# Making the marks of the attention on ScalarE, and other steps for GpSimd's splits in the first expert tile

## The chip, the cores and the metric

One core of a Trainium2 chip runs the kernel. The metric is the device time of one execution in microseconds (us). Engines: TensorE (PE; its weight loads are PEld), VectorE (DVE), ScalarE (ACT), GpSimd (POOL) and SyncE (SP), which issues DMAs. Each takes its instructions in order.

## What is computed

Three stages on B = 4 sequences of 768 tokens, 3072 tokens in all, 384 values each (8 heads of 48), all in float32: a linear attention, a mixture of 8 experts of which every token uses one, and a dense layer.

```python
for t in range(S):                               # attention
    cur = einsum('bhd,bhe->bhde', u[None] * kt, vt)
    y[:, :, t] = einsum('bhd,bhde->bhe', rt, state + cur)
    state = wt[:, :, :, None] * state + einsum('bhd,bhe->bhde', kt, vt)
...
logits = x @ w_gate + modality_bias[modality_id] # experts
e_idx = argmax(logits, axis=1)
gate_w = softmax(logits)[arange(N), e_idx]
h = maximum(x[mask] @ w1[e], 0.0)
out[mask] = gate_w[mask, None] * (h @ w2[e])
...
h = x @ w_in                                     # dense layer
out = (h * clip(h + 3.0, 0.0, 6.0) / 6.0) @ w_out
```

## The kernel before

**Attention (0 to about 187 us).** A loop over 24 steps i, each a chunk of 128 tokens of one sequence (c is the chunk in its sequence, 0 to 5). In step i TensorE forms the products of the pairs (`pairs_a`, line 830, tile aps), the new state (`update`, lines 861 and 865) and the output of the step before (`pairs_y`, 884 and 890; `take_y`, 898). VectorE prepares step i + 1 ahead of it (`prep_scan`, 775 to 779, and `prep_mult`, 788 and 789, tiles kt and pt), which TensorE's first product of step i + 1 reads. ScalarE copies: masks a_sb (837), k by tokens (kk, 851), heads and state (869, 873), the output x (899), its transpose xT (723), and it scales x by its gate before it is stored (711). GpSimd masks (839) and makes two products (z, 801, and av, 814). A few small matmuls of line 688 only fill gaps. Every engine's order is the order in which the program issues its instructions.

**Routing.** The 24 chunks form five groups (6, 6, 5, 3 and 4 chunks). Some steps after the last chunk of a group, `between()` chooses its experts (`choose`), counts, finds each token's place (`place`; plo, line 349, is its place within a row of 112) and makes the marks (`mark`, line 355): for chunk t a table of 128 tokens by 112 places, ohv, that is 0 except at the token's place, where it is the token's code (its number less 1536, plus one from the middle on, so that no code is 0; code_c). The first three groups, 17 chunks, are marked in the attention on VectorE: group 0 in steps 11 (two) and 12 (four), group 1 in steps 17, 18 and 19 (two each), group 2 in steps 22 (two) and 23 (three). `mark` is issued after the copies of k and of the factors a (`tokens_k`, `own_a`) and ahead of `take_y` and of the transposes in the same step. A matmul of the marks with a table of rows (ohh, 128 by 24 x 60, made by the large comparison of line 445) gives the index of the token in each slot: line 409 for the first expert tile, line 463 for all (24 matmuls into one sum), after which line 464 writes idx_x. The last two groups are finished within the first expert tile, by `routing_end`, a generator that is taken a step further at fixed places; there GpSimd marks five chunks and VectorE two.

**Expert tiles (about 187 to 400 us).** Seven tiles of 448 slots. Each has 8 steps f: `first(f)` (9 matmuls, tile hps, then the hidden values on ScalarE, line 589, and their rests on VectorE, line 590, tiles ring), then, two steps late, `second(f - 2)` (9 matmuls, tile acc, the third, sixth and ninth with w2l), then `side(f)`. A weight is used as a high and a low part; `split` (514, 515) makes them: a copy on ScalarE and a subtraction on VectorE or GpSimd. The table `splits` says which blocks are split in which step: in it "15" is block 5 of w1, "23" block 3 of w2. w1's block f is wanted by first(f), w2's block f by second(f). In the first tile `side(f)` issues, in this order: the routing's next step (f = 0, 1, 3), the four gathers of the next tile's tokens on GpSimd (f = 3; line 554, they read idx_x), and the splits of the step. The raw weights of the next expert are loaded into a half as soon as the half is split (line 251).

**Dense layer (to the end).** Six tiles of 512 tokens; nothing of the change lies there.

Of the kernel before, what the change touches and what calls it, by code (L numbers as in the profile page):

```python
# [9 lines left out]
F32 = mybir.dt.float32  # L10
# [5 lines left out]
AF = mybir.ActivationFunctionType  # L16
ALU = mybir.AluOpType
# [15 lines left out]
NTK = NT // 128  # L33
TM = 448
SUB = 112
NSUB = TM // SUB
# [3 lines left out]
NSLOT = NT_MAX * NSUB  # L40
# [10 lines left out]
HALF = NT // 2  # L51
# [18 lines left out]
def attention_moe_ffn(ctx, tc, wkr, v_tok, v_t, u, modality_id, w_gate, modality_bias, w1, w2, w_in, w_out, out):  # L70
    nc = tc.nc
    PE, ACT, DVE, POOL, SP = nc.tensor, nc.scalar, nc.vector, nc.gpsimd, nc.sync
    ctx.enter_context(tc.manual_schedule())

    const = ctx.enter_context(tc.tile_pool(name="const", bufs=1))
# [50 lines left out]
    iota_c = iota("iota_c", [128, SUB], [[1, SUB]], 1)  # L126
    slot_c = iota("slot_c", [128, NSLOT], [[1, NSLOT]])

    code_c = iota("code_c", [128, NTK], [[128, NTK]], -HALF, 1)
    POOL.tensor_scalar(out=code_c[:, NTK // 2:], in0=code_c[:, NTK // 2:], scalar1=1.0, scalar2=None, op0=ALU.add)  # L130
    wg_sb = const.tile([128, KD, E], F32, name="wg_sb")

    logit = keep.tile([128, NTK, E], F32, name="logit")
# [123 lines left out]
    R = {}  # L257
# [17 lines left out]
    class Route:  # L275
# [76 lines left out]
        def mark(self, js, engine):  # L352
            for j in js:
                t = self.t0 + j
                engine.tensor_scalar(out=R["ohv"][:, t, :], in0=iota_c, scalar1=self.plo[:, j:j + 1],
                                     scalar2=code_c[:, t:t + 1], op0=ALU.is_equal, op1=ALU.mult)

# [48 lines left out]
        def first_rows(self, ps):  # L406
            m = self.s.stop
            for i in range(m):
                PE.matmul(ps[0:SUB, 0:NSUB], lhsT=R["ohv"][:, i, :], rhs=self.fohh[:, i], start=(i == 0), stop=(i == m - 1))
            DVE.tensor_scalar(out=idx_x[:, 0:NSUB], in0=ps[0:SUB, 0:NSUB], scalar1=float(HALF), scalar2=None, op0=ALU.add)  # L410

        def finish(self, ps):

# [15 lines left out]
            half = self.m // 2  # L429
# [28 lines left out]
                              op1=ALU.mult)  # L458
            DVE.scalar_tensor_tensor(out=texp, in0=tef, scalar=float(E - 1), in1=own, op0=ALU.min, op1=ALU.add)
            yield  # L460
            ips = ps[0:SUB, 128:128 + NSLOT]
            for i in range(NTK):
                PE.matmul(ips, lhsT=R["ohv"][:, i, :], rhs=ohh[:, i], start=(i == 0), stop=(i == NTK - 1))
            DVE.tensor_scalar(out=idx_x, in0=ips, scalar1=float(HALF), scalar2=None, op0=ALU.add)
            yield
            after = self.tile([SUB, NSLOT], "after")
# [275 lines left out]
    with ExitStack() as actx:  # L742
# [189 lines left out]
        for i in range(n):  # L932
# [6 lines left out]
            def between():  # L939
                for part in parts:  # L940
                    at = i - part.s.stop - 3
                    if at == 0:
                        part.choose()
                    if at == 1 or (at == 0 and i == n - 1):
                        part.gates()
                        to_store.extend(range(part.s.start, part.s.stop))
                    if at == 1:
                        part.steps = part.place()
                        next(part.steps)
                        next(part.steps)  # L950
                        part.add_counts()
                    if at == 2:
                        for _ in part.steps:
                            pass
                        part.mark(range(2), DVE)
                    if at == 3:
                        part.mark(range(2, 4 if part is early else part.m), DVE)
                    if at == 4 and part is early:
                        part.mark(range(4, part.m), DVE)

            if i in (n - 4, n - 3):
                w_load(0, i - (n - 4))
# [86 lines left out]
    def routing_end():  # L1049
# [20 lines left out]
        for i in range(last.s.start, last.s.stop):  # L1070
# [6 lines left out]
    banks(pctx, reuse_waits="tile")  # L1077


    splits = {(0, 0): "22", (0, 1): "14", (0, 2): "15 23", (0, 3): "16 24", (0, 4): "17 25", (0, 5): "26",  # L1080
# [3 lines left out]
    loads = {(0, 3): 0, (0, 6): 1, (1, 2): 0, (1, 5): 1}  # L1084
# [264 lines left out]
```

## Time and profile before

| | |
|---|---|
| median of 3 runs | 825.85 us (824.87 to 825.90) |
| the profiled execution, its span | 825.67 us, 824.0 us |
| TensorE busy, of the span | 797.4 us, 97% |
| VectorE | 520.1 us, 63% |
| ScalarE | 376.8 us, 46% |
| GpSimd | 227.2 us, 28% |

The profile is one execution. A busy share is a mean over stages, so the stretches are read one by one. A row of the timeline gives the start in us, the time in us, the engine, the line, the operation, the tiles written and read and how many instructions of the kind follow each other; in brackets stands how long the engine had been idle before it, and what ended that. The granted clock is TensorE's, as a share of its full 2.4 GHz; its other level is 1.2 GHz.

### The profile page before, as it was taken

To read this page: it belongs to the slowest core of one execution; us is meant where nothing else is said; L and a number is where in the kernel's file an instruction comes from. 1 tells how busy PE (TensorE), PEld (TensorE's weight loads), DVE (VectorE), ACT (ScalarE), POOL (GpSimd) and SP (SyncE) were. 2 spreads that over 40 slices of the span, in tenths; PEclk is the share of its full clock that TensorE was granted. 3 is DMA by queue.
4 is the path that set the end of the run, shared out by engine and by line. 5 is a ranking of instruction groups with operands and counts; after the bars stand their busy time and mean duration, and the time that the engine had idled before them with its cause. 6 is when DMAs were issued, how large, how long until landed. Compare 5 with 4: busy or idle time off the path is not lost. (4 is left out here: it accounts for less than half of the span.)

```text
span 824.0 us, 16170 instructions
## 1 busy us (share of the span) xinstructions
PE 797.4 (97%) x6456; PEld 696.3 (85%) x6481; DVE 520.1 (63%) x924; ACT 376.8 (46%) x801; POOL 227.2 (28%) x240
## 2 busy tenths in 40 slices
PE   9999999999999999999999899999999999999993
PEld 4677777778999999999999799999999999999992
DVE  7789999977588989887279843433433333333331
ACT  3556677675455555554344433333333333333331
POOL 9566565655524314311012220020010002002001
PEclk9999999999999999999999999999999999999997
DMA  6797577832879877474543310110100001001001
GB/s 162 137 314 160 120 140 160 241 104 74 206 212 231 183 266 224 138 245 131 115 151 94 116 39 1 39 39 1 34 26 20 1 1 39 0 1 39 1 1 42
DMA packets 50832, 87.49 MB, mean 106 GB/s; under 512 B 11130, under 2 KB 34747, under 8 KB 50747
## 3 DMA queue, kind: packets, MB, share of 16 engines
q1 hardware_dynamic: 45147, 74.81, 33.5%
q0 software_dynamic: 4640, 11.51, 4.9%
q8 instruction: 53, 0.87, 0.5%
q14 instruction: 32, 0.26, 0.1%
q10 hardware_dynamic: 960, 0.05, 0.1%
HBM read 65.38 MB, written 20.97 MB: 105 GB/s over the span
## 5 line engine op out<-in xcount | busy, mean ns | idle before, releaser
L511 PE MATMUL hps<-xin,wih 128*128 128x512 f32 x576 | 179.1, 392 | 0.0
L632 DVE SCALAR_TENSOR_TENSOR r<-r,hps 128x512 f32<-128x512 f32 (+1 forms) x97 | 66.1, 681 | 164.5 <-ACT r L631 164.5
L511 PE MATMUL acc<-woh,ring 128*128 128x384 f32 x576 | 163.9, 339 | 2.2 <-DVE ring L636 2.2
L631 ACT ACTIVATE r<-hps,three 128x512 f32<-128x512 f32 (+1 forms) x97 | 66.3, 683 | 167.2 <-PE hps L511 166.7
L511 PEld LDWEIGHTS hps<-xin,wih 128*128 128x128 f32 x576 | 106.8, 188 | 17.7
L511 PE MATMUL hps<-xin,wil 128*128 128x512 f32 x288 | 113.9, 396 | 0.0
L671 POOL DMA_INDIRECT out<-zo,order x24 | 24.8, 1033 | 315.5 <-ACT zo L668 310.0
L511 PEld LDWEIGHTS acc<-woh,ring 128*128 128x128 f32 x576 | 105.5, 188 | 7.4 <-DVE ring L636 3.2
L636 DVE SCALAR_TENSOR_TENSOR ring<-r,ring 128x512 fp32r<-128x512 f32 (+1 forms) x97 | 67.0, 691 | 59.2 <-ACT ring L635 59.1
L511 PE MATMUL hps<-xin,w1h 128*128 128x448 f32 x336 | 98.2, 373 | 0.0
L511 PE MATMUL acc<-wol,ring 128*128 128x384 f32 x288 | 96.9, 336 | 0.0
L511 PE MATMUL acc<-ring,w2h 128*128 128x448 f32 x336 | 95.8, 366 | 0.0
L635 ACT ACTIVATE ring<-r 128x512 fp32r<-128x512 f32 (+1 forms) x97 | 60.7, 626 | 64.0 <-DVE r L632 64.0
L515 POOL TENSOR_TENSOR w2l<-w2r,w2h 128x384 fp32r<-128x384 f32 x33 | 36.9, 1123 | 126.3 <-ACT w2h L514 126.3
L511 PEld LDWEIGHTS acc<-ring,w2h 128*128 128x128 f32 x336 | 63.5, 189 | 4.7
L511 PEld LDWEIGHTS hps<-xin,w1h 128*128 128x128 f32 x336 | 61.8, 189 | 4.2 <-DVE xin L563 0.2
L511 PE MATMUL tps<-woh,ring 128*128 128x384 f32 x192 | 64.0, 334 | 0.0
L511 PEld LDWEIGHTS hps<-xin,wil 128*128 128x128 f32 x288 | 54.0, 187 | 11.5
L511 PE MATMUL hps<-xin,w1l 128*128 128x448 f32 x168 | 61.5, 366 | 0.0
L511 PE MATMUL acc<-ring,w2l 128*128 128x448 f32 x168 | 61.3, 365 | 0.0
L589 ACT ACTIVATE ring<-hps 128x448 fp32r<-128x448 f32 x56 | 30.4, 543 | 63.1 <-PE hps L511 62.9
L511 PEld LDWEIGHTS acc<-wol,ring 128*128 128x128 f32 x288 | 54.1, 188 | 4.1
(237 smaller groups left out, 1347.7 us busy)
## 6 DMA issues: line engine op xcount, KB each, us to landing
wkr<-in_wkr SPq DMA_DIRECT2D x42, 288.9 KB, 5.0
w1r<-in_w SPq DMA_DIRECT2D x14, 768.0 KB, 6.1
w2r<-in_w SPq DMA_DIRECT2D x14, 768.0 KB, 8.3
raw<-in_w_in SPq DMA_DIRECT2D x12, 512.0 KB, 8.1
raw<-in_w_out SPq DMA_DIRECT2D x16, 384.0 KB, 3.1
yt_dram<-yst SPq DMA_DIRECT2D x7, 672.0 KB, 7.3
v_sb<-in_v_tok SPq DMA_DIRECT2D x24, 192.0 KB, 5.6
yt_dram<-warm_sb SPq DMA_DIRECT2D x3, 1536.0 KB, 9.6
```

The source lines that it names most:

```text
L511: PE.matmul(ps, lhsT=lt, rhs=rt, start=(start and q == 0), stop=(stop and q == last))
L515: sub.tensor_tensor(out=l, in0=raw, in1=f32(h), op=ALU.subtract)
L589: ACT.activation(out=hh, in_=ps, func=AF.Relu)
L631: ACT.activation(out=r6[:, s], in_=ps[:, s], func=AF.Relu, bias=three)
L632: DVE.scalar_tensor_tensor(out=r6[:, s], in0=r6[:, s], scalar=6.0, in1=ps[:, s], op0=ALU.min, op1=ALU.mult)
L635: ACT.activation(out=gh[:, s], in_=r6[:, s], func=AF.Copy, scale=1.0 / 6.0)
L636: DVE.scalar_tensor_tensor(out=gl[:, s], in0=r6[:, s], scalar=1.0 / 6.0, in1=f32(gh[:, s]), op0=ALU.mult, op1=ALU.subtract)
L671: ins = POOL.indirect_dma_start(out=out[:, :], out_offset=bass.IndirectOffsetOnAxis(ap=order[:, s:s + 1], axis=0), in_=zo, in_offset=None, ...
```

## The change

The marks of the attention are made on ScalarE: the square of the distance of the token's place from each column, then max(0, code - code x square), which is the code at distance 0 and 0 elsewhere. This needs positive codes, so the codes of the first half of the tokens change sign (code_c) and a table of negative codes is added (code_n), both made by GpSimd ahead of its other work. The sign is put back where codes are read: line 410 multiplies by -1; in `finish` the 24 matmuls form two sums, one for each half of the tokens, one is copied, and their difference is the index. In the first expert tile the splits move to other steps: "14 22" in step 0, none in steps 1 and 2, "15 23" in step 3, and the later ones one step on. `split_w1` there uses GpSimd for f < 3 and VectorE afterwards, as before, so w1's block 5 goes from GpSimd to VectorE.

```diff
 
     code_c = iota("code_c", [128, NTK], [[128, NTK]], -HALF, 1)
     POOL.tensor_scalar(out=code_c[:, NTK // 2:], in0=code_c[:, NTK // 2:], scalar1=1.0, scalar2=None, op0=ALU.add)
+
+    POOL.tensor_scalar(out=code_c[:, :NTK // 2], in0=code_c[:, :NTK // 2], scalar1=-1.0, scalar2=None, op0=ALU.mult)
+    code_n = const.tile([128, NTK], F32, name="code_n")
+    POOL.tensor_scalar(out=code_n, in0=code_c, scalar1=-1.0, scalar2=None, op0=ALU.mult)
     wg_sb = const.tile([128, KD, E], F32, name="wg_sb")
 
     logit = keep.tile([128, NTK, E], F32, name="logit")
...
         def mark(self, js, engine):
             for j in js:
                 t = self.t0 + j
+                if engine is ACT:
+
+                    far = self.pool.tile([128, SUB], F32, name="far", bufs=1)
+                    ACT.activation(out=far, in_=iota_c, func=AF.Square, scale=-1.0, bias=self.plo[:, j:j + 1])
+                    ACT.activation(out=R["ohv"][:, t, :], in_=far, func=AF.Relu, scale=code_n[:, t:t + 1],
+                                   bias=code_c[:, t:t + 1])
+                    continue
                 engine.tensor_scalar(out=R["ohv"][:, t, :], in0=iota_c, scalar1=self.plo[:, j:j + 1],
                                      scalar2=code_c[:, t:t + 1], op0=ALU.is_equal, op1=ALU.mult)
 
...
             m = self.s.stop
             for i in range(m):
                 PE.matmul(ps[0:SUB, 0:NSUB], lhsT=R["ohv"][:, i, :], rhs=self.fohh[:, i], start=(i == 0), stop=(i == m - 1))
-            DVE.tensor_scalar(out=idx_x[:, 0:NSUB], in0=ps[0:SUB, 0:NSUB], scalar1=float(HALF), scalar2=None, op0=ALU.add)
+            DVE.tensor_scalar(out=idx_x[:, 0:NSUB], in0=ps[0:SUB, 0:NSUB], scalar1=-1.0, scalar2=float(HALF), op0=ALU.mult,
+                              op1=ALU.add)
 
         def finish(self, ps):
 
...
                               op1=ALU.mult)
             DVE.scalar_tensor_tensor(out=texp, in0=tef, scalar=float(E - 1), in1=own, op0=ALU.min, op1=ALU.add)
             yield
-            ips = ps[0:SUB, 128:128 + NSLOT]
+            half = [ps[0:SUB, o:o + NSLOT] for o in (128, 256)]
             for i in range(NTK):
-                PE.matmul(ips, lhsT=R["ohv"][:, i, :], rhs=ohh[:, i], start=(i == 0), stop=(i == NTK - 1))
+                PE.matmul(half[i >= NTK // 2], lhsT=R["ohv"][:, i, :], rhs=ohh[:, i], start=(i % (NTK // 2) == 0),
+                          stop=(i % (NTK // 2) == NTK // 2 - 1))
+            low = self.tile([SUB, NSLOT], "low")
+            DVE.tensor_copy(low, half[0])
+            ips = self.tile([SUB, NSLOT], "ips")
+            DVE.tensor_tensor(out=ips, in0=half[1], in1=low, op=ALU.subtract)
             DVE.tensor_scalar(out=idx_x, in0=ips, scalar1=float(HALF), scalar2=None, op0=ALU.add)
             yield
             after = self.tile([SUB, NSLOT], "after")
...
                     if at == 2:
                         for _ in part.steps:
                             pass
-                        part.mark(range(2), DVE)
+                        part.mark(range(2), ACT)
                     if at == 3:
-                        part.mark(range(2, 4 if part is early else part.m), DVE)
+                        part.mark(range(2, 4 if part is early else part.m), ACT)
                     if at == 4 and part is early:
-                        part.mark(range(4, part.m), DVE)
+                        part.mark(range(4, part.m), ACT)
 
             if i in (n - 4, n - 3):
                 w_load(0, i - (n - 4))
...
     banks(pctx, reuse_waits="tile")
 
 
-    splits = {(0, 0): "22", (0, 1): "14", (0, 2): "15 23", (0, 3): "16 24", (0, 4): "17 25", (0, 5): "26",
-              (0, 6): "27 10 11", (0, 7): "12 13 20",
+    splits = {(0, 0): "14 22", (0, 1): "", (0, 2): "", (0, 3): "15 23", (0, 4): "16 24", (0, 5): "17 25",
+              (0, 6): "26 27 10 11", (0, 7): "12 13 20",
               (1, 0): "21 22 14", (1, 1): "23 15", (1, 2): "16 24", (1, 3): "17 25", (1, 4): "26 10", (1, 5): "27 11 20",
               (1, 6): "12 21", (1, 7): "13 22", (2, 0): "23 14 24"}
     loads = {(0, 3): 0, (0, 6): 1, (1, 2): 0, (1, 5): 1}
```

## Rows read from the trace of the kernel before

**Rows 1.** Busy us of each engine in a stretch, granted clock, DMA share
```profile
100.00:160.20 60.20, 55.94 (x1122) 43.42 (x1130) 58.32 (x103) 41.49 (x114) 37.32 (x37) 1.00 0.73 162
```

**Rows 2.** Timeline, TensorE, its waits for VectorE in the attention
```profile
107.01 0.71 PE L830 MATMUL aps<-pt,kt 48*128 48x128 f32 x8 [0.87 <-DVE pt L789]
...
144.43 0.71 PE L830 MATMUL aps<-pt,kt 48*128 48x128 f32 x8 [0.93 <-DVE pt L789]
...
150.96 0.71 PE L830 MATMUL aps<-pt,kt 48*128 48x128 f32 x8 [0.67 <-DVE pt L789]
...
159.65 0.38 PE L688 MATMUL ups<-warm_sb 128*128 128x512 bf16 x1 [0.81 <-DVE idx_x L410]
```

**Rows 3.** Timeline, VectorE, two groups of marks
```profile
137.51 0.58 DVE L355 TENSOR_SCALAR ohv<-iota_c,plo,code_c 128x112 f16<-128x112 f32 x2
...
150.73 2.16 DVE L355 TENSOR_SCALAR ohv<-iota_c,plo,code_c 128x112 f16<-128x112 f32 x2
```

**Rows 4.** ScalarE by form to 187 us: count, busy us, mean ns, idle before
```profile
L711 ACT ACTIVATE x_keep<-x_keep,gate 128x384 f32<-128x384 f32 x19 | 10.9, 608 | 0.0
...
L514 ACT ACTIVATE w1h<-w1r 128x384 fp32r<-128x384 f32 x2 | 1.0, 515 | 0.0
...
L300 ACT ACTIVATE ex<-lsub 128x24 f32<-128x24 f32 x1 | 0.2, 223 | 0.0
```

**Rows 5.** Busy us of each engine in two stretches around later marks
```profile
174.08:186.73 12.65, 12.65 (x233) 9.96 (x236) 7.03 (x21) 10.46 (x28) 4.44 (x6) 1.00 0.25 82
135.43:151.10 15.67, 13.93 (x284) 10.50 (x288) 15.19 (x29) 11.06 (x28) 10.54 (x12) 1.00 0.78 169
```

**Rows 6.** Timeline, the end of the attention on ScalarE and TensorE
```profile
176.21 1.61 ACT L711 ACTIVATE x_keep<-x_keep,gate 128x384 f32<-128x384 f32 x3
...
186.73 0.49 ACT L899 ACTIVATE x_keep<-yps 128x384 f32<-128x384 f32 x1
...
187.64 0.49 PE L720 MATMUL tps<-ident,x_keep 128*128 128x128 f32 x3
```

**Rows 7.** Timeline, places of group 1, and a copy that TensorE reads
```profile
136.72 0.75 DVE L349 SCALAR_TENSOR_TENSOR plo<-phw,rsel 128x6 f32<-128x6 f32 x1
...
149.33 0.55 ACT L851 ACTIVATE kk<-tps 128x448 f32<-128x448 f32 x1
...
152.11 0.67 PE L865 MATMUL ups<-v_sb,kk 128*64 128x48 f32 x16
```

**Rows 8.** Timeline, GpSimd and VectorE at the start
```profile
4.14 1.13 POOL L130 TENSOR_SCALAR code_c<-code_c 128x12 f32<-128x12 f32 x1
...
5.26 1.77 DVE L777 TENSOR_SCALAR tot<-pt 112x4 f32<-112x4 f32 x1
```

**Rows 9.** Timeline, the first expert tile around the large comparison
```profile
195.28 1.28 DVE L355 TENSOR_SCALAR ohv<-iota_c,plo,code_c 128x112 f16<-128x112 f32 x2
...
197.88 1.99 POOL L515 TENSOR_TENSOR w1l<-w1r,w1h 128x384 fp32r<-128x384 f32 x2
...
198.06 0.87 DVE L443 SCALAR_TENSOR_TENSOR phi<-phi,phw 128x24 f32<-128x24 f32 x1
...
198.97 2.42 DVE L445 TENSOR_TENSOR ohh<-slot_c,phi 128x1440 f16<-128x1440 f32 x1
...
201.43 1.38 PE L463 MATMUL tps<-ohh,ohv 128*112 128x60 f16 x24 [1.46 <-DVE ohh L445]
```

**Rows 10.** Busy us and granted clock behind the comparison, and in the dense layer
```profile
202.00:208.00 6.00, 6.00 (x35) 5.52 (x34) 3.91 (x11) 1.37 (x3) 2.88 (x4) 0.72 0.42 146
...
500.00:600.00 100.00, 100.00 (x503) 90.57 (x502) 37.71 (x56) 35.16 (x56) 4.19 (x4) 1.00 0.08 24
```

**Rows 11.** Timeline, the index, GpSimd behind the gathers, and second(3)'s third matmul
```profile
204.26 0.20 DVE L464 TENSOR_SCALAR idx_x<-tps 112x60 int32<-112x60 f32 x1
...
209.57 2.97 POOL L515 TENSOR_TENSOR w2l<-w2r,w2h 128x384 fp32r<-128x384 f32 x3
...
210.19 0.36 PE L511 MATMUL acc<-ring,w2l 128*128 128x448 f32 x1
```

## Prediction, made before the changed kernel was run

> **What bounds the kernel now.** I read the engine table and the slices first: TensorE is busy for 97% of the span, so only three kinds of time can be won: TensorE's waits, its slow clock, and work of its own. The change touches no TensorE work but a split of one sum. Then I read the busy times by stretch, in which TensorE and VectorE are both nearly full in the second half of the attention [rows 1]: two engines in step, so an idle moment of TensorE there is VectorE being late. The timeline names these moments: four waits of TensorE on VectorE between 100 and 160 us, 0.87, 0.93, 0.67 and 0.81 us, together 3.28 us [rows 2]. All other iterations there run at TensorE's own pace. The second place is the first expert tile: TensorE waits 1.46 us for the large comparison, and a stretch at a lower clock follows [rows 9, 10]. After about 220 us TensorE is full, and nothing of the change lies there.
>
> A forecast is made against the profiled execution: 825.67 us, a span of 824.0 and 1.67 around it; the median of the runs is 825.85, so the two are the same within 0.2 us. What a measurement of this kernel can tell from no change is about 0.2%, 1.65 us.
>
> **Marks leave VectorE.** 17 marks (6, 6 and 5 tokens' tiles in three groups) go. Two of them take 0.58 us when GpSimd leaves VectorE alone and 2.16 us when it doesn't [rows 3]. The excess is a wait which the next VectorE instruction may inherit, so I count 0.29 us a mark for sure: 17 x 0.29 = 4.9 us of VectorE. It is worth only what TensorE waited for, at most 3.28 us: each of the four waits has marks of 0.58 us or more among the instructions of VectorE in the one or two iterations ahead of it, and with those gone VectorE comes early enough for most of each. Bounds: 0.58 us each where the freed time goes into another wait for GpSimd (four times, 2.3 us, or as little as 1 us if the late ones inherit it), and 3.28 us.
>
> **Marks come to ScalarE.** The trace has no such instruction, so I build one: 24 columns take 223 ns and 384 take 515 ns, 0.81 ns a column, so 112 columns take 294 ns; a scale per partition adds 608 - 515 = 93 ns [rows 4]. Square has one such operand (387 ns), Relu two (480 ns): 0.87 us a mark. Neighbours on ScalarE overlap by (3 x 0.608 - 1.61) / 2 = 0.11 us [rows 6], but Relu reads what Square writes. I take 0.85 (0.65 to 0.87). That is 17 x 0.85 = 14.5 us for the 4.9 us taken off VectorE.
>
> The Trainium skill speaks against such an exchange: in "ScalarE: Activation LUTs", Rules for kernel authors, plain arithmetic belongs on VectorE. Its section What ACT_TABLE_LOAD costs gives 186 ns + 0.833 ns a column + 93 ns per pointer operand, by which a mark would take an estimated 0.84 us less an overlap; the rows above agree.
>
> Does ScalarE have room? It is a queue in order, so I look where marks stand and what is behind them. Group 0 (two, then four marks): ScalarE idles there and nobody waits soon; nothing. Group 1: the first two marks wait for the places, which VectorE finishes at 136.72 + 0.75 = 137.47 us, while ScalarE is free for them from 135.43: 2.04 us of standing, with four marks by 151.1 that is 2.04 + 3.4 = 5.4 us against 15.67 - 11.06 = 4.6 us of idle time [rows 5, 7]. Behind them stand the copies of x, the masks and the copy of k; that copy ends at 149.88 and TensorE takes it at 152.11, a slack of 2.2 us [rows 7]. 0.8 of it goes to the lateness and 1.6 to TensorE's own two gains there (0.93 + 0.67): 0.2 short. Not all idle time can be used, so I take 0.5 us off the gain (0 to 1).
>
> Group 2 is worse. Its five marks fall in the last two iterations: 5 x 0.85 = 4.25 us, against 12.65 - 10.46 = 2.19 us of idle time on ScalarE from 174.08 to 186.73 [rows 5]. So ScalarE ends the attention 2.06 us late. Behind the marks stand the copies of the last x, the first x to be split and the transposed x; the last copy of x ends at 187.22 and TensorE transposes it at 187.64 [rows 6], a slack of 0.2 to 0.4. So TensorE loses **1.8 us** there (0.6 at 0.65 us a mark, 2.3 if the idle time is poorly used). VectorE had nothing late there, so nothing is won against it.
>
> **GpSimd's two constants.** Two more small instructions stand ahead of the memsets. Alone such ones take about 0.2 us; the one there now takes 1.13 us beside a scan, and a VectorE instruction of four elements takes 1.77 us until the memsets are over [rows 8]. Behind them on GpSimd's queue stand the bias of the router, the first product z (own_z) and the first masks, for which TensorE's first iteration waits. I take 0.5 us (-0.5, if VectorE slips in between the two dependent instructions, to 1.2, if one is held like its neighbour).
>
> **Code sums.** The two sums are 24 matmuls as before; two VectorE instructions of 60 columns are added ahead of the index, of some 0.2 us each, as the index itself takes [rows 11]. The gathers wait for them, and what waits for the gathers is below.
>
> **The first tile.** Now VectorE's chain meets GpSimd's subtractions: an instruction of 24 columns takes 0.87 us and ends as the first subtraction does, and the comparison takes 2.42 us, beginning while the second runs to 199.87 [rows 9]. Without them they would end about 0.7 + 0.9 us sooner. Against that: one more weight copy (0.4 to 0.5 us) now stands ahead of the copy of the hidden values on ScalarE (ring, line 589), which VectorE's chain follows; and the two subtractions of the first step now run back to back while VectorE's own two marks (1.28 us beside one subtraction [rows 9]) want to start, up to 0.8 us more. So the comparison ends between 200.2 and 201.2 instead of 201.39, and the wait of 1.46 us shrinks to between 0.3 and 1.25.
>
> The Trainium skill, "GPSIMD Engine Reference", Specifications, says that GpSimd shares its SBUF interfaces with VectorE, and that instructions with two SBUF inputs contend. The trace agrees for the subtractions; by that rule GpSimd's own marks, which now end near 199, would hold the chain too, and the wait would be the long one.
>
> The clock that falls behind the wait (a mean of 0.72 granted from 202 to 208, between its two levels) cost some 6 x (1 - 0.72) = 1.7 us [rows 10]. That may go. But the subtraction of w2's block 3 now stands on GpSimd behind the four gathers, which wait for the index and occupy GpSimd until 209.57 [rows 11]; the index, and they, come 0.3 to 1.1 us earlier after the change, so block 3's subtraction, 1 us, ends at 209.4 to 210.2. TensorE wants it in the third matmul of second(3), at 210.19 before [rows 11]. With wait and slow clock gone it would be there sooner: the sums end at 201.6 to 202.5, then 9 + 9 + 9 + 2 matmuls of 100 / 503 = 0.2 us [rows 10] make 207.4 to 208.3. So a new wait of about 1.9 us takes the place of the old one and takes most of the gain back; I keep **0.4 us** of gain (3.1 if the wait did not come, a loss of 1.5 if the clock falls behind it as well). The block's raw weights are also freed later for the next load, which has some 10 us.
>
> **Sum.** -3.3 + 0.5 + 1.8 + 0.5 - 0.4 = -0.9: 825.67 - 0.9 = **824.8 us**.
>
> **Rivals.** (1) *The marks are cheap*: Square and Relu overlap or idle time takes them, 0.6 us lost at the end instead of 1.8, nothing at the start, and the slow clock goes for 1.1 us more: about 822.0. For it: ScalarE is the least full of the three in the attention. Against: the last two iterations. Chance 0.33.
> (2) *Slower through block 3*: the wait behind the gathers is long enough for the clock to fall again. This decides once TensorE arrives over 1.5 us ahead of the subtraction, since the wait of 1.46 us was followed by the slow clock [rows 9, 10]. The tile then loses 1.5 instead of gaining 0.4, and with ScalarE's end at 2.3 and the start at 1.2 the time is 825.67 - 2.8 + 2.3 + 1.2 + 1.5 = 827.9. For it: the order on GpSimd's queue. Against: GpSimd may get its indices earlier. Chance 0.20.
> (3) *VectorE gains nothing*: the freed time is inherited as waits for GpSimd, 1 us won instead of 3.3, the rest as in the sum: 827.1. For it: the marks' times of 2.16 against 0.58. Against: the 0.58 themselves. Chance 0.10.
> My forecast has 0.37.
>
> **Chances and range.** Faster by over 0.2% is below 824.2: rival 1 and a small part of the forecast, 0.37. Slower is above 827.5: most of rival 2 and a part of 3, 0.22. The same: 0.41. The range holds the ends of the terms of the forecast, most of rival 1 and up to rival 2: 821.6 to 828.0.
>
> **What would show it.** In the profile after: no wait of TensorE on VectorE's prepared tiles after 100 us (right) or the same four (rival 3); ScalarE pairs of 0.39 and 0.48 us; ScalarE without idle time from 174 us and TensorE waiting on its copies of x at the turn into the first tile; the comparison near 1.7 us; a wait of TensorE on GpSimd's subtraction of w2 right after the gathers; the granted clock at 200 to 212 us. The forecast is wrong if TensorE doesn't wait at the end of the attention, or if block 3 is ready in time.

## The result, and the profile after

The changed kernel takes 835.38 us (median of 4 runs, 834.06 to 836.67) against 825.88 us (4 runs, 824.87 to 826.81): 1.0117 times as long, 95% interval 1.0102 to 1.0132. The forecast was 824.8 us with a range to 828.0, so it was wrong, by 10.6 us. The profiled execution took 835.98 us with a span of 834.2, 10.2 more than the 824.0 of before. (Some executions of experiments, and of the kernel before beside them, lay far above the others and are left out of the ratios; so each experiment is given by its profiled execution, with its ratio to the kernel before where that has an interval.)

Where the 10.2 us are: I read the start of landmarks from the timelines (TensorE's first `aps` product of an iteration, which is a step i of the attention's loop, the first product of the first expert tile, ScalarE's first copy of each tile's y) and took differences, in us. "First tile" runs from its first product to its first y copy, "tiles 2 to 7" on to the seventh tile's. The same table serves all experiments.

| kernel | iterations 0 to 21 | 21 to 23 | 23 to first product | first tile | tiles 2 to 7 | span |
|---|---|---|---|---|---|---|
| before | 150.10 | 15.10 | 11.65 | 39.71 | 182.75 | 824.0 |
| after | 147.74 | 16.77 | 17.97 | 42.26 | 184.68 | 834.2 |
| e1 marks, old splits | 147.66 | 16.82 | 17.96 | 42.27 | 184.69 | 833.9 |
| e2 splits only | 149.81 | 15.10 | 11.65 | 39.19 | 182.76 | 824.0 |
| e3 third group on VectorE | 147.69 | 21.07 | 11.75 | 40.42 | 184.77 | 829.6 |
| e4 codes and sums only | 149.73 | 15.09 | 11.65 | 40.25 | 184.68 | 827.0 |
| e5 block 3 early | 147.64 | 21.23 | 13.23 | 38.93 | 184.77 | 830.0 |
| e6 other order | 147.65 | 16.80 | 16.05 | 41.80 | 185.51 | 833.2 |
| e7 tile of 128 bytes | 147.84 | 16.61 | 17.94 | 42.03 | 181.11 | 829.9 |
| e8 before, 96 bytes more | 149.71 | 15.09 | 11.65 | 39.74 | 184.68 | 824.4 |
| e9 gathers later | 147.93 | 15.08 | 13.88 | 40.25 | 184.78 | 826.0 |
| e10 before, 128 bytes more | 149.72 | 15.09 | 11.65 | 39.64 | 181.12 | 822.2 |
| e11 three edits | 147.56 | 15.08 | 11.65 | 40.32 | 181.11 | 820.5 |
| e12 and block 3 early | 148.96 | 15.08 | 11.65 | 38.77 | 181.11 | 819.6 |

After against before: -2.4, +1.7, +6.3, +2.6 and +1.9, which is 10.1; the first iteration begins 0.5 later and the dense layer's part is 0.4 shorter, together the 10.2. The first iteration begins anywhere from 9.4 to 10.8 us in these kernels, at 10.78 in e2, which has the old codes, and at 10.53 in the changed kernel: nothing can be said of the two constants from it. The two instructions took 0.26 and 0.28 us on GpSimd, and its first product z, which stands behind them, began at 12.88 us instead of 13.48, so no delay of it is seen.

TensorE's waits in the changed kernel from 100 to 230 us (engine, line, tile waited for, engine and line that released it, us, times, longest):

```profile
PE lps L737 <- DVE logit L757: 3.3, 1, 3.3
PE acc L528 <- POOL w2l L532: 2.1, 1, 2.1
PE ups L705 <- DVE rk L342: 1.3, 1, 1.3
PE tps L475 <- DVE ohh L457: 1.2, 1, 1.2
```

The four waits of [rows 2] are gone. Of the waits in this list, the first and the third are new in the attention (the third is a wait of filler matmuls for VectorE's ranks, tile rk, in iteration 21), the second is new in the first tile, and the fourth is that of [rows 9], 1.46 us before. The stretches that answer to [rows 1], [rows 5] and [rows 10] (length; busy us and instructions of TensorE, weight loads, VectorE, ScalarE, GpSimd; granted clock, DMA share, GB/s), then the stretch behind the comparison, which the changed kernel reaches 6.4 us later, and two behind the new waits:

```profile
100.00:160.20 60.20, 59.54 (x1160) 45.04 (x1160) 56.02 (x98) 48.35 (x135) 34.30 (x37) 1.00 0.73 168
174.08:186.73 12.65, 10.09 (x186) 7.73 (x184) 3.47 (x13) 10.98 (x30) 4.22 (x6) 1.00 0.19 63
202.00:208.00 6.00, 4.75 (x28) 4.17 (x27) 5.79 (x14) 3.07 (x7) 3.27 (x4) 1.00 0.37 132
...
208.00:217.00 9.00, 7.15 (x52) 6.35 (x50) 5.60 (x14) 2.74 (x6) 4.70 (x5) 1.00 0.47 152
...
188.00:194.00 6.00, 6.00 (x61) 4.55 (x60) 1.90 (x5) 3.21 (x9) 0.00 (x0) 0.50 0.29 101
219.00:221.00 2.00, 2.00 (x7) 1.75 (x6) 1.79 (x11) 0.00 (x0) 0.08 (x1) 0.50 0.93 326
```

In the 60 us that [rows 1] show, VectorE is busy 2.3 us less, ScalarE 6.9 more and TensorE 3.6 more: the exchange works as meant there, though the two kernels are up to 2.4 us apart by then and the stretches don't hold quite the same work. Behind the 3.3 us wait TensorE runs at half its clock (0.50, that is 1.2 GHz) from about 187.3 to 194 us, and again behind the 2.1 us wait.

The price of a mark on ScalarE, by form up to 188 us (count, busy us, mean ns):

```profile
L363 ACT ACTIVATE ohv<-far,code_c,code_n 128x112 f16<-128x112 f32 x17 | 8.2, 480 | 0.6
L362 ACT ACTIVATE far<-iota_c,plo 128x112 f32<-128x112 f32 x17 | 6.6, 387 | 4.3 <-DVE plo L353 3.9
```

387 and 480 ns are the sums made from [rows 4], to the nanosecond. The chain to TensorE's 3.3 us, from the timelines of ScalarE, VectorE and TensorE:

```profile
182.64 0.39 ACT L362 ACTIVATE far<-iota_c,plo 128x112 f32<-128x112 f32 x1
183.06 0.48 ACT L363 ACTIVATE ohv<-far,code_c,code_n 128x112 f16<-128x112 f32 x1
183.57 0.39 ACT L362 ACTIVATE far<-iota_c,plo 128x112 f32<-128x112 f32 x1
...
185.32 0.20 ACT L304 ACTIVATE ex<-lsub 128x24 f32<-128x24 f32 x1
185.43 0.47 ACT L916 ACTIVATE x_keep<-yps 128x384 f32<-128x384 f32 x1
185.80 0.48 ACT L740 ACTIVATE xT<-lps 128x384 f32<-128x384 f32 x1
...
185.56 0.18 DVE L315 TENSOR_REDUCE esum<-ex 128x3 f32<-128x24 f32 x1 [5.33 <-ACT ex L304]
186.72 0.56 DVE L532 TENSOR_TENSOR w1l<-w1r,w1h 128x384 fp32r<-128x384 f32 x1 [0.58 <-ACT w1h L531]
187.20 0.16 DVE L757 TENSOR_TENSOR logit<-lps,bias_t 128x8 f32<-128x8 f32 x1
...
187.50 0.87 PE L737 MATMUL lps<-ident,x_keep 128*128 128x128 f32 x3 [3.33 <-DVE logit L757]
```

A mark takes 0.93 us from start to start (183.57 - 182.64): Relu waits for Square, and there is a gap besides. The next Square waits for the Relu too: the kernel gives `far` a single buffer. A second one was not tried. Behind the last three marks stand the exponential and the copies of x and of its transpose. VectorE, idle for 5.33 us, takes what they leave: a sum, a split of weights, and at the end the addition of the logits, which reads the bank `lps` that TensorE's next transposes want. That is the wait. Before, the same transposes began without one:

```profile
183.87 0.49 PE L720 MATMUL lps<-ident,x_keep 128*128 128x128 f32 x3
```

### The profile page after: what moved, and what is told of

The parts are those of the page before. It is cut to its first block, busy times and chain, and to the rows that moved or that the text cites. A ratio compares the mean times of both kernels' runs of the same rounds, so it can differ in the third digit from the quotient of the medians.

```text
span 834.2 us, 16211 instructions
## 1 busy us (share of the span) xinstructions
PE 807.3 (97%) x6481; PEld 698.6 (84%) x6481; DVE 514.0 (62%) x910; ACT 389.3 (47%) x835; POOL 222.1 (27%) x241
## 5 line engine op out<-in xcount | busy, mean ns | idle before, releaser
L528 PEld LDWEIGHTS hps<-xin,wih 128*128 128x128 f32 x576 | 106.8, 188 | 17.8
L528 PEld LDWEIGHTS hps<-xin,wil 128*128 128x128 f32 x288 | 54.0, 188 | 11.5
```

What stands on the lines that cost most here:

```text
L528: PE.matmul(ps, lhsT=lt, rhs=rt, start=(start and q == 0), stop=(stop and q == last))
```

## The experiments

**e1_marks: the change without its new splits.**

```diff
-    splits = {(0, 0): "14 22", (0, 1): "", (0, 2): "", (0, 3): "15 23", ...
+    splits = {(0, 0): "22", (0, 1): "14", (0, 2): "15 23", (0, 3): "16 24", ...
```

> The change with the old table of splits: marks on ScalarE, new codes and two sums. Theory A (ScalarE's queue): the five marks of group 2 stand at the end of the attention, ScalarE comes some 3 us late, TensorE waits about 3.3 us there, the clock falls behind that, and the first expert tile starts some 6 us late: about 832 us. Theory B (the splits: the wait for block 3 of w2 and the clock behind it carry the loss): about 827 us.

Measured: 835.64 us in the profiled execution; 1.0181 times before [1.0091, 1.0272]. That is above both expected times. The waits in the attention are those of the changed kernel, 3.3 us for the logits and 1.7 for the ranks, so the attention's loss comes with the marks. The first tile is as long as in the changed kernel, but made up otherwise: no wait for block 3, and a low clock behind the 3.3 us wait that reaches four microseconds into the tile (0.50 from 193 to 197 us) instead of one. Equal lengths here don't show that the splits cost nothing; e2 is the run that tells.

**e2_splits: the kernel before with the new splits.**

```diff
-    splits = {(0, 0): "22", (0, 1): "14", (0, 2): "15 23", ...
+    splits = {(0, 0): "14 22", (0, 1): "", (0, 2): "", (0, 3): "15 23", ...
```

> The kernel before with the new table of splits alone. Theory A: the comparison ends earlier, but TensorE waits about 2 us for block 3's subtraction behind the gathers and the clock falls there: 826 to 828.5 us. Theory B: at least 832 us.

Measured: 825.86 us, ratio 0.9994 [0.9983, 1.0005]. The wait for the comparison is 1.3 us instead of 1.46, a wait of 1.1 us for block 3's subtraction appears, the clock stays at 1.00 from 200 to 220 us, and the first tile is 0.5 us shorter. Alone, the splits are no change that can be measured. Theory A's wait came at half its size and without the low clock; theory B is out.

**e3_group2: the third group's five marks back on VectorE.**

```diff
-                        part.mark(range(2), ACT)
+                        part.mark(range(2), DVE if part.g == 2 else ACT)
```

(and the same at `mark` of the next iteration.)

> The changed kernel with the marks of group 2 (steps 22 and 23) made on VectorE again, those of groups 0 and 1 on ScalarE. Theory A: no wait of 3.3 us at the end of the attention and no slow clock behind it; 6 us of the loss gone, about 829 us. If instead GpSimd's and VectorE's interference in step 21 (a product of 3.93 us instead of 1.12) carries the loss, it stays above 833 us.

Measured: 831.36 us, ratio 1.0073 [1.0036, 1.0109]. The 3.3 us wait is gone and the way from iteration 23 to the first product is 11.75 us, that of before. So it was those marks. But the 1.7 us wait in iteration 21 was followed by the low clock in this execution, and iteration 22 took 11.5 us instead of 7.2.

**e4_sums: positive codes and the two sums alone, all marks on VectorE, old splits.**

```diff
-                        part.mark(range(2), ACT)
+                        part.mark(range(2), DVE)
```

(at all three places.)

> The new codes (two GpSimd instructions at the start) and the two sums alone: all marks of the attention on VectorE, the old splits. Theory A: 0.5 us from the start and 0.2 to 0.4 from the later index: 826 to 827 us. Rival: the sums' longer way to the index delays the gathers so that the second tile waits: 829 us or more.

Measured: 828.76 us, ratio 1.0048 [1.0020, 1.0077]. The attention is that of before. The first tile is 0.5 us longer, with two waits of together 1.5 us for gathered rows that come later: counted from the tile's first product, the index is begun at 17.8 us instead of 17.3, and the first gather at 18.8 instead of 17.8. The clock stays at 1.00 from 200 to 220 us, and these waits take up what that gives. The other 1.9 us are in tiles 2 to 7, where no instruction of the kernel differs. All kernels run so far with the new constant tile show them (184.7 us), e2 doesn't (182.76). That asked for e7 and e8.

**e7_pad: the changed kernel with its new constant tile 32 columns wide instead of 24,** 128 bytes of a partition instead of 96.

```diff
-    code_n = const.tile([128, NTK], F32, name="code_n")
+    code_n = const.tile([128, 32], F32, name="code_n")[:, :NTK]
```

> The changed kernel with one edit: its new constant tile is allocated 32 columns wide instead of 24 (128 bytes of a partition instead of 96), so that every tile allocated behind it moves by a whole 128 bytes and stands as in the kernel before with respect to 64 bytes. Theory M (place in memory): the 1.93 us that the six later expert tiles lost (182.75 us from the first to the seventh y copy before, 184.68 after, and 184.7 in every kernel with the new tile) come from the 96 bytes by which the operands moved; then this run shows 182.7 to 182.9 us for these tiles and comes out about 1.9 us below the changed kernel, at 833.2 to 833.9. Theory W (the work changed): the two part sums or the marks cost the tiles something, and 184.7 stays, with a time of 835.2 to 835.8. The 3.3 us wait for the logit copy at the end of the attention stays under both.

**e8_shift: the kernel before with such a tile of 96 bytes, which nothing reads.**

```diff
+    code_n = const.tile([128, NTK], F32, name="code_n")
+    POOL.tensor_scalar(out=code_n, in0=code_c, scalar1=-1.0, scalar2=None, op0=ALU.mult)
```

> The kernel before with one edit: the new constant tile (24 columns, 96 bytes of a partition) is allocated and filled where the changed kernel has it, and nothing reads it. Theory M: the expert tiles take 184.7 us from the first to the seventh y copy instead of 182.75, and the time is 1.9 us above the kernel before, 827.5 to 828.2 us. Theory W: 182.75 stays, and the time is that of the kernel before within 0.5 us.

**e10_shift128: the kernel before with an unread tile of 128 bytes.**

```diff
+    code_n = const.tile([128, 32], F32, name="code_n")
+    POOL.memset(code_n, 0.0)
```

> The kernel before with one edit: an unread constant tile of 128 bytes of a partition is allocated (cleared once by GpSimd) where the changed kernel has its new tile of 96. Theory M128 (the pitch of the products depends on where the tiles stand, and 128 bytes further it is lower than in either kernel): the six later expert tiles take 181.1 us from the first to the seventh y copy as in the padded changed kernel (30.04 each), against 182.75 here before, and the time falls by about 1.6 us, to 824.2 to 824.9. Rival L (the 181.1 of the padded kernel comes from its other changes, and only 32 bytes against 0 within 64 count): 182.7 to 182.8 stay, with the time of the kernel before within 0.5 us.

Measured: e7 831.59 us, ratio 1.0056 [1.0036, 1.0076]; e8 826.14 us profiled, ratio 1.0018 [1.0007, 1.0029]; e10 823.96 us, ratio 0.9967 [0.9953, 0.9981]. Tiles 2 to 7 take 181.11, 184.68 and 181.12 us: the place in memory alone costs 1.9 us or gives 1.6, whatever the marks do. (e8's time lies below the one expected since its start, attention and dense layer were together 1.5 us shorter in this execution.) The pitch of the products, from start to start, shows it. TensorE's timeline in a later tile of before, after and e7, the first and the last row of nine products, from `acc` to the next `hps`:

```profile
320.64 0.57 PE L511 MATMUL acc<-ring,w2h 128*128 128x448 f32 x2
...
322.46 0.57 PE L511 MATMUL hps<-xin,w1h 128*128 128x448 f32 x2
```
```profile
319.18 0.57 PE L528 MATMUL acc<-ring,w2h 128*128 128x448 f32 x2
...
321.02 0.37 PE L528 MATMUL hps<-xin,w1h 128*128 128x448 f32 x1
```
```profile
320.52 0.56 PE L528 MATMUL acc<-ring,w2h 128*128 128x448 f32 x2
...
322.32 0.56 PE L528 MATMUL hps<-xin,w1h 128*128 128x448 f32 x2
```

Nine products of 448 columns take 1.82, 1.84 and 1.80 us: 202, 204 and 200 ns each. e7's expectation was 182.7 us, the time of before, since 128 bytes seemed to leave everything standing as it stood; the tiles came out shorter than in the kernel before, and e10's did too. In the dense layer the pitch does not move: the products of `wih`, 512 columns, have a mean of 229.7 ns in before, after, e7, e8 and e10 alike. So theory M holds in that place decides in the expert tiles, but not in its rule: which operand's place matters, and modulo what, is open and wasn't tried.

**e9_gathers: the first two row gathers of the first tile one iteration later.**

```diff
-GATHERS = {20: (0, 1), 21: (2,), 22: (3,)}
+GATHERS = {21: (0, 1), 22: (2, 3)}
```

> The changed kernel with one edit: the first two row gathers of the first tile are issued a step later (four gathers in steps 21, 21, 22, 22 instead of 20, 20, 21, 22). Theory G (GpSimd's unbroken row of a gather, two additions and a further operation holds VectorE's product of the ranks): the wait of 1.3 us of TensorE for that product in step 21 falls to below 0.4, the product takes 1.1 to 1.5 us instead of 3.93, and the step from the start of step 21 to that of step 22 takes about 7.9 us instead of 9.6; the run comes out 1 to 1.7 us below the changed kernel unless the row returns in the next step. Rival S (the wait comes from ScalarE's marks that delay what VectorE waits for): 1.3 to 1.7 stay.

The wait in iteration 21 in the changed kernel, from the timelines of VectorE, TensorE, GpSimd and ScalarE. TensorE waits for `rk`, the ranks, a short instruction that stands behind VectorE's product `pt` (line 806) in its queue; the product that took 3.93 us is `pt`:

```profile
162.72 3.93 DVE L806 TENSOR_TENSOR pt<-wkr,pt 112x512 f32<-112x512 f32 x1
...
167.11 0.16 DVE L342 TENSOR_TENSOR rk<-ups,oh 128x40 f32<-128x40 f32 x1
...
167.31 0.59 PE L705 MATMUL ups<-warm_sb 128*128 128x512 bf16 x2 [1.29 <-DVE rk L342]
...
161.69 1.15 POOL L571 DMA_INDIRECT xg<-x_dram,idx_x  x1 [0.30 <-issue]
162.85 1.23 POOL L856 TENSOR_SCALAR_AFFINE_SELECT a_sb<-a_sb 128x512 f32<-128x512 f32 x2
164.05 1.26 POOL L818 TENSOR_TENSOR z<-wkr 112x512 f32<-112x512 f32 x1
165.28 0.82 POOL L831 TENSOR_TENSOR av<-v_sb,a_tok 128x384 f32<-128x384 f32 x1
...
173.37 1.99 DVE L353 SCALAR_TENSOR_TENSOR plo<-phw,rsel 128x5 f32<-128x5 f32 x1
...
175.39 0.39 ACT L362 ACTIVATE far<-iota_c,plo 128x112 f32<-128x112 f32 x1 [1.54 <-DVE plo L353]
```

and in e9 VectorE's product, GpSimd's masks, and TensorE's wait at the end of the attention:

```profile
161.88 0.68 DVE L806 TENSOR_TENSOR pt<-wkr,pt 112x512 f32<-112x512 f32 x1
...
161.87 1.77 POOL L856 TENSOR_SCALAR_AFFINE_SELECT a_sb<-a_sb 128x512 f32<-128x512 f32 x2 [3.52 <-ACT a_sb L854]
...
183.55 0.52 PE L737 MATMUL lps<-ident,x_keep 128*128 128x128 f32 x3 [2.04 <-DVE logit L757]
```

Measured: 827.76 us in the profiled execution, 833.25 in another; there is no ratio with an interval. The product takes 0.68 us instead of 3.93, the wait in iteration 21 is gone (theory G), and 21 to 23 takes 15.1 us as before. In the changed kernel GpSimd goes from a gather into two masks, a product and another product without a pause, and VectorE's product, which now comes earlier, starts inside that row and ends 0.55 us behind its last instruction. Before, and again in e9, GpSimd stood idle ahead of the masks, and the product began together with them: 1.12 us before, 0.68 in e9, though masks and products follow without a pause there too. In these three kernels only the start inside the row costs:

```profile
161.90 0.97 POOL L554 DMA_INDIRECT xg<-x_dram,idx_x  x1 [0.30 <-issue]
164.38 1.67 POOL L839 TENSOR_SCALAR_AFFINE_SELECT a_sb<-a_sb 128x512 f32<-128x512 f32 x2 [1.52 <-ACT a_sb L837]
...
164.44 1.12 DVE L789 TENSOR_TENSOR pt<-wkr,pt 112x512 f32<-112x512 f32 x1
```

The Trainium skill, "SBUF — State Buffer", section SBUF: two separate sides, says that GpSimd and a VectorE instruction with two SBUF inputs, as this one, hold their shared ports as a lock for one whole instruction and that the loser blocks; here the loser was held through the rest of a gather and three following entries of the timeline, more than one instruction.

There is more to e9: the wait for the logits shrank too, from 3.33 to 2.04 us, with the clock at 1.00 behind it. The 1.29 us of difference came from the late places: in the changed kernel `plo` took 1.99 us beside GpSimd (0.55 in e9), ScalarE stood still for 1.54 us and was that much later with its marks of both iterations. Counted from the start of iteration 23, TensorE's transposes begin at 8.6 us before, 10.8 in e9 and 12.5 in the changed kernel, and from there to the tile's first product it takes 3.1, 3.1 and 5.5 us.

**e6_queue: the changed kernel with the last parts' work ordered otherwise,** so that the exponential stands ahead of the marks and the logits' addition ahead of the second weight split.

```diff
-                for part in parts:
+                for part in reversed(parts):
...
-            if i >= n - 2:
-                split_w1(i - (n - 2))
+            if i == n - 2:
+                split_w1(0)
+            if i == n - 1:
+                logits_add(*pairs)
+                split_w1(1)
...
-        logits_add(*pairs)
```

> The changed kernel with the order in the last step altered: the parts are taken from the last to the first, so that the gates of the last part stand in ScalarE's queue ahead of the marks of the second, and VectorE's addition of the last logits stands ahead of its second split of the weights. Theory Q (the second part's three marks hold ScalarE's exponential, that holds VectorE's sum and all behind it in its queue, and the logits addition at its end keeps the bank that TensorE's transposes want): the wait of 3.3 us of TensorE for the logits addition falls to 1 us or less, the way from the start of step 23 to the first product of the first tile shortens from 17.97 us to 12 to 15, TensorE's clock stays above 0.9 of full or falls for under 2 us, and the time is 830 to 833 us. Rival C (ScalarE's copies behind the marks are what TensorE waits for, as the prediction had it): 2 us or more stay in one wait, now named after a copy of ScalarE, and the time is 834 to 836.

ScalarE's copy, VectorE's addition and TensorE's transposes in e6:

```profile
185.99 0.48 ACT L740 ACTIVATE xT<-lps 128x384 f32<-128x384 f32 x1
...
186.50 0.17 DVE L757 TENSOR_TENSOR logit<-lps,bias_t 128x8 f32<-128x8 f32 x1 [2.73 <-ACT xT L740]
...
186.73 0.55 PE L737 MATMUL lps<-ident,x_keep 128*128 128x128 f32 x3 [2.37 <-DVE logit L757]
```

Measured: 834.87 us, ratio 1.0138 [1.0067, 1.0208]. With VectorE's queue empty the wait is still 2.37 us: the addition, and with it TensorE, waits for ScalarE's copy of the transpose behind the marks. So of 3.33 us VectorE's queue had 0.96 and ScalarE's own copies the rest. Theory Q explains the smaller part; rival C, which is the prediction's own mechanism, the larger.

**e5_block3: block 3 of the first tile split ahead of the gathers.**

```diff
-    splits = {(0, 0): "14 22", (0, 1): "", (0, 2): "", (0, 3): "15 23", ...
+    splits = {(0, 0): "14 22", (0, 1): "", (0, 2): "23", (0, 3): "15", ...
```

> The changed kernel with one edit: in the list of splits of the first tile the third block's second-matrix split goes to place 2 and its first-matrix split to place 3, where the changed kernel has both at place 3, so that GpSimd subtracts for block 3 before it issues the row gathers of the next tile. Theory B (the subtraction of block 3 waits behind the gathers): TensorE's wait of 2.07 us for it falls below 0.7, the clock stays at 1.00 of full between 217 and 222, and the way from the first place product to the first y copy shortens from 27.5 us to 24.9 to 25.5; the time falls by about 2 us, to 833.0 to 834.0. Rival T (the tile is bound by its gathered rows or its weights anyway): the wait goes and another one of the tile takes its place, 26.5 us or more stay, and the time falls by less than 1 us.

The wait in the changed kernel, GpSimd's last gather and the subtractions behind it, then, earlier in the tile, two small steps of VectorE beside GpSimd's subtractions, the comparison that follows them, and TensorE's wait for it:

```profile
215.20 0.94 POOL L571 DMA_INDIRECT xg<-x_dram,idx_x  x1 [0.30 <-issue]
216.17 2.91 POOL L532 TENSOR_TENSOR w2l<-w2r,w2h 128x384 fp32r<-128x384 f32 x3
...
217.22 0.47 PE L528 MATMUL acc<-ring,w2l 128*128 128x448 f32 x1 [2.07 <-POOL w2l L532]
...
201.78 1.00 DVE L439 TENSOR_TENSOR tre<-tpe,tst 128x8 f32<-128x8 f32 x1
...
202.85 0.93 DVE L446 TENSOR_TENSOR_SCAN tcum<-ones_f,tre 128x8 f32<-128x8 f32 x1
...
206.08 1.66 DVE L457 TENSOR_TENSOR ohh<-slot_c,phi 128x1440 f16<-128x1440 f32 x1
...
207.79 1.38 PE L475 MATMUL tps<-ohh,ohv 128*112 128x60 f16 x24 [1.25 <-DVE ohh L457]
```

Measured: 831.67 us, ratio 1.0086 [1.0057, 1.0115]. The wait is gone, and from the place products (L475) to the first y copy it takes 24.38 us instead of 27.48: theory B, and 3.1 us rather than 2, since the low clock behind the wait goes with it. The total fell by more than that in the profiled execution (two others took 834.26 and 835.39, so it says little), but parts moved besides: in this execution the low clock came behind the wait of iteration 21,

```profile
172.00:178.00 6.00, 6.00 (x72) 4.33 (x72) 0.00 (x0) 3.26 (x9) 3.49 (x4) 0.50 0.12 34
```

and the attention's end, with ScalarE having had time to catch up, waited 1.4 us and kept its clock.

**e11_sum and e12_sum3: the repairs together.** e11 is the changed kernel with e3, e7 and e9's edits; e12 has e5's besides.

> The changed kernel with three edits together: the third group's marks back on VectorE, the first two row gathers of the first tile a step later, and the new constant tile 128 bytes wide. By the sum of the single runs: step 23 begins 163.0 us after the first step (165.2 before), the way from there to the first product of the first tile is 11.7 us as before with no wait for the logits, and TensorE's clock stays at 1.00 of full through it (-2.2 us together); the first tile is as before within 0.5 us; the later six tiles take 181.1 us (-1.6): 821.5 to 823 us, 0.996 of the kernel before. If VectorE's five marks collide again with GpSimd or the clock falls, 824 to 826.

> The kernel with the three edits and, besides, block 3 of the first tile split ahead of the gathers. Theory B: the wait for block 3's subtraction (0.5 to 1.1 us where the clock stays up) goes, and the time is 0.5 to 1 us below the kernel with the three edits. Rival T: the same time within 0.3 us.

Measured: e11 822.26 us (ratio 0.9926 [0.9845, 1.0008]), e12 821.32 us, ratio 0.9942 [0.9923, 0.9962]. TensorE's waits in e12 from 100 to 230 us:

```profile
PE tps L475 <- DVE ohh L457: 1.6, 1, 1.6
PE lps L752 <- issue: 0.7, 1, 0.7
PE hps L528 <- DVE w1l L532: 0.5, 1, 0.5
```

e11's time came out at its sum: 2.5 us from the attention and 1.6 from the place of the tiles, with 0.6 lost in the first tile, where at most 0.5 was expected. e12 takes 1.5 us off the first tile and loses 1.4 on the way to iteration 21, with a wait of 1.3 us for a logits addition between 45 and 65 us, ahead of all marks, that e11 did not have. e12 is below the kernel before; e11 is in its profiled execution, but its interval reaches 1.0008. Of e12's 4.35 us (825.67 - 821.32) the tiles' place gives 1.6, which has nothing to do with the marks. The fair mate is e10, the kernel before with the same 128 bytes: 823.96 us, so 1.7 us are left to e11's edits and 2.6 to e12's.

## Why the prediction was wrong, step by step

**Marks leave VectorE: right.** The sum had 3.3 us less 0.5 for ScalarE, 2.8; all four waits went, and iteration 21 is reached 2.4 us sooner (2.0 sooner than in e4, which has the same codes).

**Their price on ScalarE: right, slightly small.** 0.387 + 0.480 us as built from the rows; the pitch of 0.93 us lies above the upper bound of 0.87 that I set, since the Relu reads what the Square writes, and here two such neighbours leave a gap instead of overlapping.

**ScalarE's queue at the end of the attention: the mechanism right, the term mis-sized.** This is the term that failed. It stands in the sum with 1.8 us and measured 6.3. The marks by themselves cost 2.2 us (e9, 13.88 - 11.65), near the 1.8. The places that came late from iteration 21 added 1.7 (12.5 against 10.8 us to the transposes), and the half clock behind the wait of 3.33 us 2.4 (5.5 against 3.1 us from there to the tile). The wait also fell one step ahead of the place that the prediction read its slack from: not at the transposes of the last x, but at those before them, over the bank `lps` and VectorE's addition of the logits. The failing step was to ask for the clock only in the first tile, and to take the stretch as if VectorE handed over its places on time. "VectorE had nothing late there, so nothing is won against it" was true of before and not of after.

**What the earlier VectorE runs into: a step that wasn't made.** With the gain, GpSimd's pause between gather and masks went, and VectorE's product started inside the row instead of together with the masks. Rival 3 named the mechanism (freed time inherited as waits for GpSimd) but only as a smaller gain; it is a loss of 1.7 us in its iteration, and of the other 1.7, just named, two iterations later (e9 against after).

**The first tile: the sum took the wrong one of two branches.** The comparison took 1.66 us as forecast (about 1.7) and the wait 1.25, the long end of 0.3 to 1.25: two of the small steps ahead of the comparison took 1.00 and 0.93 us beside the two subtractions, the contention which the prediction cites the Trainium skill ("GPSIMD Engine Reference", Specifications) for. Beside GpSimd's own marks, which the prediction feared by that rule as well, such steps took some 0.2 us, as they do alone. The wait behind the gathers came with 2.07 us for a forecast of 1.9, and was over the 1.5 us from which rival 2 let the clock fall, which it did. That 2.07 is so near 1.9 is in part luck: counted from the tile's first product, TensorE was there at 22.1 us and the subtraction done at 24.2, where the working has 20.5 to 21.4 and 22.5 to 23.3; both were late. The sum booked a gain of 0.4, rival 2 a loss of 1.5; it is 2.6, of which some 0.5 is the attention's low clock, still there in the tile's first microsecond. The credit of 1.7 us for the clock behind the comparison came (1.00 from 208 to 217 us) and was paid again behind the gathers. In e2 and e4 the clock stays up throughout, and yet the tile is only 0.5 us shorter and 0.5 longer than before, as other waits take the credit's place (1.1 us for block 3, 1.5 us for gathered rows).

**The constants and the code sums: small, one of them put too low.** Of the 0.5 us for GpSimd's constants no run shows anything beyond the scatter of the start. The two sums were taken as two instructions of 0.2 us with an index that comes sooner; they put the first gather back by 1.0 us (e4), only half of it through the later index, and where the other half comes from is open.

**Tiles 2 to 7: no step at all.** "Nothing of the change lies there" was said of the instructions. The new tile moved every operand by 96 bytes, and that cost 1.9 us (e8).

**Open.** What decides whether the clock falls behind a wait: 2.04 us (e9) and 1.1 us (e2) were not followed by the low clock, 3.33 and 2.07 us (the changed kernel) and 2.37 us (e6) were, and of four executions with 1.7 us in iteration 21 two were (e3, e5) and two not (e1, e6). Ahead of the place products, the 1.46 us of before were and the 1.5 us of e5 were not.

## What to carry to other kernels

Work moved to a queue in order must be paid at that queue's tightest stretch, and a wait that it makes is to be priced with the slow clock that can follow it: some 2.9 us behind the wait of 3.33 here (2.4 and 0.5), and some 1.7 behind that of 2.07, where the clock was at 0.50 for about 3.4 us. An engine that gets faster arrives elsewhere: check what runs on its neighbour at the new time. Before believing a small difference in a stretch that the edit doesn't touch, shift the memory by an unread tile; a pad of 128 bytes gave 1.6 us here, as much as the 1.7 that e11's edits gave besides it.

## What the runs showed of the hardware that I had not expected

TensorE's pitch for the same products of the expert tiles depends on where the tiles stand in memory: 202 ns before, 204 with 96 bytes more, 200 with 128 more, at a granted clock of 1.00, while the dense layer's products keep theirs. The Trainium skill, "TensorE: Matmul & The Clock Gate", section Back-to-back issue gap, gives N / 2.4 + 2.5 ns for an isolated matmul, by which 448 columns would take an estimated 189 ns, says that a stream of wide ones takes less, and has no part for the place; the streams here took more.

A VectorE instruction that takes 0.68 us in e9 took 3.93 us in the changed kernel, where it started during a gather of GpSimd and ended behind the last of several instructions that GpSimd ran without a pause.
